# First head pair of a clustered attention and mixture kernel: centroid norms by Newton steps alone, identity matmuls in TensorE's pauses, seven exchange transfers, shared evictions, and GpSimd's split held back

## The chip, the cores and the metric

The kernel runs on one core of one Trainium2 chip. The metric is the device time of one execution in microseconds; where several runs are given, the median counts. The core's engines work from queues of their own: TensorE (PE; its weight loads are shown as PEld), VectorE (DVE), ScalarE (ACT), GpSimd (POOL) and SyncE (SP), which here only issues transfers. ScalarE and GpSimd can issue transfers too.

## What is computed

Inputs are q, k, v of shape (2, 8, 768, 64), 16 centroids per head, and the weights of two feed-forward stages. The attention lets a query see a key only if both fall into the same cluster:

```python
q_n = q / (norm(q) + 1e-06)
k_n = k / (norm(k) + 1e-06)
c_n = centroids / (norm(centroids) + 1e-06)
q_assign = argmax(einsum('bhsd,hcd->bhsc', q_n, c_n), -1)
k_assign = argmax(einsum('bhsd,hcd->bhsc', k_n, c_n), -1)
mask = q_assign[:, :, :, None] == k_assign[:, :, None, :]
scores = where(mask, scale * q @ k.T, -1e9)
attn = softmax(scores)
x = (attn @ v) reshaped to (1536, 512)
x = leaky_relu(x @ w_in) @ w_out
out = gated mixture of 8 experts on x, with a skip gate
```

An argmax over clusters does not depend on the length of q or k, so the kernel normalizes the centroids only.

## The kernel before

The attention works on eight pairs (a batch and two heads each), with 12 steps per pair in a software pipeline of 96 steps (the loop `for s in range(NSTEP + 12 + LAG)`). A step takes 128 queries of one head: `st_scores` makes the 128x768 scores on TensorE (tile `sps`), VectorE takes the row maximum (`st`), ScalarE the exponential (`pr`), TensorE transposes it (`tps`), ScalarE evicts that (`pt`), and a few steps later TensorE multiplies by v (`avps`). Scores have nearly f32 accuracy from operands split into a high and a low part. For the first head of a pair they lie in U = `UA` and V = `VA`, for the second in `UB` and `VB`; each tile has 128 partitions and a q and a k part. In U the high part stands in partitions 0 to 63 and the cluster mask, 16 rows of large numbers, from 64 on; V holds the parts for the two correction products. Since the two heads of a pair arrive in different partition halves, parts move between halves by transfers in SBUF: the exchange.

The preparation of a pair: transposes of the loaded q and k on TensorE (`raw_pe`, tile `rawps`), evictions (`raw_act`, tile `raw`), the cluster scores (`assign_pe`, tile `asps`), their eviction (`sc`), transposes (`argmax_pe`, tile `scps`), four VectorE passes for a one-hot of the argmax (`argmax_0` to `argmax_3`: `mx`, `eq`, `eq`, `mx`, `oh`), and the mask rows. For later pairs a table (`plan`, `PREPS`) spreads these over the steps of the pair before. For pair 0 there is nothing to hide behind: it is written out in line ahead of the step loop, and each engine's queue has the order in which these statements stand. That is where nearly all of the change lies.

Before, in this opening: SyncE issues the loads of q (tile `first`), the centroids (`cnat`), k (`first`), then q and k of pair 1. `first_copy` brings q and k into the layout for the transposes, one half on ScalarE, the other on VectorE (q) or GpSimd (k). `prep_centroids` takes the norms: square (`csq`), sum, a square root on ScalarE, two Newton steps on VectorE, reciprocal, and the scaled centroids (`cexp`); `prep_cblk` transposes these on TensorE (`cps`) and copies them to `cblk`, the weights of `asps`. `first_hi` makes the high parts (GpSimd for q, ScalarE for k), `first_lo` the low parts (VectorE). Then the exchange, nine transfers of 192 KB, eight on SyncE's queue and one on GpSimd's. `mask_first` makes the mask rows by 24 small transposes (`mps`), evicted by ScalarE (keys) and VectorE (queries). Pair 1 is transposed and evicted during the argmax; `split_first(1, i)` splits it on GpSimd and starts its exchange.

Of the kernel before, what the change touches and what calls it, by code (L numbers as in the profile page):

```python
# [25 lines left out]
def kernel(  # L26
# [14 lines left out]
    nc = tc.nc  # L41
# [51 lines left out]
    def load_qk(p):  # L93
        b, cc = divmod(p, NPAIR)
        for nm, src in (("q", q), ("k", k)):
            if p:
                t = att_a.tile([P, NT, 2, D], F32, tag="nat" + nm, name="nat" + nm)
                nat[nm, p] = t
                nc.sync.dma_start(t, src[b, 2 * cc:2 * cc + 2].rearrange("h (p t) d -> p t h d", t=NT))
            else:  # L100
                t = att.tile([P, 2, HS], F32R, tag="pr", name="first", bufs=4)
                t = _f(t.rearrange("p a b -> p (a b)")).rearrange("p (h t d) -> p h t d", h=2, d=D)
                nc.sync.dma_start(t, src[b, 0:2].rearrange("h (p t) d -> p h t d", t=NT))
                first[nm] = t
                nat[nm, 0] = nat0[:, "qk".index(nm)]
            if p == 0 and nm == "q":
                nc.sync.dma_start(cnat, centroids.rearrange("h c d -> (h c) d"))

# [27 lines left out]
    nc.vector.memset(warm, 1.0)  # L136
    nc.scalar.activation(out=warm, in_=warm, func=AF.Sqrt)
    nc.vector.tensor_single_scalar(pid, pid, NC_, op=ALU.bitwise_and)
# [4 lines left out]
    def prep_centroids():  # L143
# [3 lines left out]
        nc.vector.tensor_reduce(out=st[:, 0:1], in_=sq, axis=AX.X, op=ALU.add)  # L147
        first_copy(1)
        nc.scalar.activation(out=st[:, 1:2], in_=st[:, 0:1], func=AF.Sqrt)
        nc.vector.tensor_scalar(out=st[:, 1:2], in0=st[:, 1:2], scalar1=1e-30, scalar2=None, op0=ALU.max)  # L150
        for i in (1, 2):
            nc.vector.reciprocal(out=st[:, 3:4], in_=st[:, i:i + 1])
            nc.vector.scalar_tensor_tensor(out=st[:, 3:4], in0=st[:, 0:1], scalar=st[:, 3:4], in1=st[:, i:i + 1],
                                           op0=ALU.mult, op1=ALU.add)
            nc.vector.tensor_scalar(out=st[:, 2 * i:2 * i + 1], in0=st[:, 3:4], scalar1=0.5, scalar2=1e-6 * (i - 1),
                                    op0=ALU.mult, op1=ALU.add)
# [30 lines left out]
    def raw_act(p, i):  # L187
        qk, half = divmod(i, 2)
        ps = ps_prep.pop(("raw", i)).rearrange("p j c -> p (j c)")
        sc = SCALE if qk == 0 else 1.0  # L190
        nc.scalar.activation(out=raw_t[p][:, i, :], in_=ps, func=AF.Copy, scale=sc)

# [8 lines left out]
    def raw_split(p, i):  # L201
# [5 lines left out]
        lo = (VA if qk == 0 else VB)[:, qk, cs]  # L207
        nc.gpsimd.tensor_scalar(out=hi, in0=raw[:, i, :], scalar1=1.0, scalar2=1.0, op0=ALU.mult, op1=ALU.mult)
        nc.gpsimd.tensor_tensor(out=lo, in0=raw[:, i, :], in1=_f(hi), op=ALU.subtract)
# [57 lines left out]
    def argmax_3(p):  # L267
# [3 lines left out]
        oh_t[p] = oh  # L271

    def mask_first(h):
        U = uv_t[0][h]
        for qk in (1, 0):
# [8 lines left out]
            else:  # L284
                for cs in (slice(0, HS), slice(HS, S)) if h == 0 else (slice(0, S),):
                    nc.vector.tensor_scalar(out=U[64:64 + NC_, 0, cs], in0=ps[:, cs], scalar1=BIG, scalar2=-BIG,
                                            op0=ALU.mult, op1=ALU.add)

# [180 lines left out]
    def first_copy(i):  # L469
        nm = "qk"[i // 2]  # L470
        ts_ = slice(3 * (i % 2), 3 * (i % 2) + 3)
        for h in range(2):
            src, dst = first[nm][:, h, ts_, :], nat[nm, 0][:, ts_, h, :]
            if h:
                nc.scalar.activation(out=dst, in_=src, func=AF.Copy)
            elif nm == "q":
                nc.vector.tensor_copy(dst, src)
            else:
                nc.gpsimd.tensor_scalar(out=dst, in0=src, scalar1=1.0, scalar2=1.0, op0=ALU.mult, op1=ALU.mult)

    first_copy(0)
    prep_centroids()
    first_copy(2)
    first_copy(3)
    for i in range(4):
        raw_pe(0, i)
        raw_act(0, i)
    for i in range(4):
# [4 lines left out]

    def first_lo(qk, halves=(0, 1)):
        for half in halves:
            cs = slice(half * HS, (half + 1) * HS)
# [3 lines left out]
    Uq, Wq, Xq, Yq = (_f(t[:, 0, :]) for t in (UA, UB, VA, VB))  # L500
    Uk, Wk, Xk, Yk = (_f(t[:, 1, :]) for t in (UA, UB, VA, VB))
    nc.sync.dma_start(Wq[0:64], Uq[64:128])
    nc.sync.dma_start(Yq[64:128], Uq[64:128])
    nc.sync.dma_start(Wk[0:64], Uk[64:128])
    nc.sync.dma_start(Yk[0:64], Uk[64:128])
    first_lo(0, (0,))
    prep_cblk()
    first_lo(0, (1,))
    nc.sync.dma_start(Yq[0:64], Xq[64:128])
    nc.gpsimd.dma_start(Xk[0:64], Uk[0:64])  # L510
    assign_pe(0)
    first_lo(1)
    lo_kf = _f(lo_k.rearrange("p a b -> p (a b)"))
    nc.sync.dma_start(Xk[64:128], lo_kf[0:64])
    nc.sync.dma_start(Yk[64:128], lo_kf[64:128])
    nc.sync.dma_start(Xq[64:128], Uq[0:64])
    prep(0, 3, "a0")
    nc.scalar.activation(out=warm, in_=warm, func=AF.Exp)
    prep(0, 3, "pb")
    for r in range(4, 7):  # L520
        for slot in ("d", "pb"):
            prep(0, r, slot)
    load_v(0)
    for i in range(4):
        raw_pe(1, i)
        raw_act(1, i)
    load_qk(2)
    mask_first(0)
# [160 lines left out]
    for s in range(NSTEP + 12 + LAG):  # L689
        p, r = divmod(s, 12)  # L690
        if s < NSTEP:
            st_scores(s)
        conv_step(s, 0)
        preps(p, r, "a0")
# [929 lines left out]
```

## Time and profile before

| | us |
|---|---|
| median of 3 runs | 648.55 |
| lowest and highest | 646.94, 648.65 |
| the profiled execution's own time | 648.61 |
| its span, first to last instruction | 646.9 |
| TensorE busy in it | 626.0 |
| VectorE, ScalarE, GpSimd busy | 481.5, 415.5, 164.1 |

The profile is of one execution. Its times count from the start of the span. In a timeline a line is a group of like instructions that follow each other: start, time from the first start to the last end, engine, source line, operation, what it writes and reads, the number of instructions, and the idle time before it with what ended it. In the chain of waits a line is a piece of the path that ended last: start, length, engine or transfer, and the source line.

### The profile page before, as it was taken

The page shows a single profiled execution, that of the slowest core. Times are in us where ns is not written, and L with a number is a line of the kernel's source. Part 1 is how long each engine was busy: PE and PEld are TensorE (multiplying, and loading weights), DVE is VectorE, ACT ScalarE, POOL GpSimd, SP SyncE. Part 2 cuts the span into 40 slices and gives each one's busy share as a digit, 9 for nine tenths or more (in the row PEclk, how much of TensorE's full clock was granted, in tenths as well). Part 3 has the DMA queues.
Part 4 walks back from the last instruction along what each step waited for, and adds up shares of the span by engine and source line. Part 5 has one row for each costly group of instructions (what it writes and reads, how often), then busy time and mean ns, then how long its engine had stood idle before and what let it go on. Part 6 is the DMA issues. An engine that isn't in the chain of part 4 may idle for free.

```text
span 646.9 us, 10034 instructions
## 1 busy us (share of the span) xinstructions
PE 626.0 (97%) x3505; PEld 485.7 (75%) x3505; DVE 481.5 (74%) x893; ACT 415.5 (64%) x817; POOL 164.1 (25%) x215
## 2 busy tenths in 40 slices
PE   5999999999999999999999999999998999999994
PEld 3776777776776775888888888888886878688874
DVE  6757778787868653988766888767988548999961
ACT  5788898988888885655544444445453346688860
POOL 3333647463746333400000000000000125005111
PEclk9999999999999999999999999999998999999998
DMA  7766566578666518233014211017353438999940
GB/s 187 181 188 169 137 158 196 150 198 188 193 185 165 169 33 315 79 117 98 3 35 146 98 42 39 17 50 261 133 195 126 141 131 305 368 362 363 359 137 28
DMA packets 66246, 104.26 MB, mean 161 GB/s; under 512 B 27994, under 2 KB 32060, under 8 KB 65810
## 3 DMA queue, kind: packets, MB, share of 16 engines
q1 hardware_dynamic: 62914, 95.36, 47.5%
q0 software_dynamic: 3280, 8.24, 3.9%
q8 instruction: 28, 0.46, 0.3%
q14 instruction: 24, 0.20, 0.1%
HBM read 77.45 MB, written 12.72 MB: 139 GB/s over the span
## 4 chain that ended last, share of the span: by engine, by line
PE 83%; DVE 7%; ACT 3%; DMA 2%; POOL 2%; issue 2%; SPq 0%; POOLq 0%; DVEq 0%
PE ups L669 17%; PE acc L775 16%; PE sps L371 10%; PE avps L443 9%; PE tps L428 8%; PE hps L1315 7%; PE yps L1346 7%; DVE ohe L881 2%; PE rawps L179 1%; ACT pr L389 1%; PE hT L1327 1%; PE acc L1207 1%; PE asps L232 1%; DVE gl L762 1%; DMA stg<-in_moe_w_in_dram 1%
## 5 line engine op out<-in xcount | busy, mean ns | idle before, releaser
L374 DVE TENSOR_REDUCE st<-sps 128x1 f32<-128x768 f32 x96 | 91.6, 955 | 52.2 <-PE sps L371 51.2
L435 ACT ACTIVATE pt<-tps 128x384 f32<-128x384 f32 x192 | 85.4, 509 | 18.6 <-PE tps L428 17.4
L389 ACT ACTIVATE pr<-sps,st 128x768 f32<-128x768 f32 x96 | 87.9, 916 | 10.0 <-DVE st L374 9.8
L428 PE MATMUL tps<-ident,pr 128*128 128x128 f32 x576 | 79.1, 273 | 0.5 <-ACT pt L435 0.5
L669 PE MATMUL ups<-xh,whii 128*128 128x512 f32 x192 | 74.9, 390 | 0.0
L669 PE MATMUL ups<-xh,wloi 128*128 128x512 f32 x192 | 74.7, 389 | 0.0
L669 PE MATMUL ups<-xl,whii 128*128 128x512 f32 x192 | 74.7, 389 | 0.0
L775 PE MATMUL acc<-whio,gh 128*128 128x512 f32 x183 | 72.8, 398 | 0.0
L428 PEld LDWEIGHTS tps<-ident,pr 128*128 128x128 f32 x576 | 67.8, 140 | 5.9 <-ACT pt L435 1.8
L443 PE MATMUL avps<-pt,vnat 128*64 128x384 f32 x384 | 72.1, 498 | 0.0
L775 PE MATMUL acc<-whio,gl 128*128 128x512 f32 x183 | 71.7, 392 | 0.0
L775 PE MATMUL acc<-wloo,gh 128*128 128x512 f32 x183 | 71.7, 392 | 0.0
L760 ACT ACTIVATE gh<-g 128x512 fp32r<-128x512 f32 x48 | 30.4, 633 | 59.5 <-DVE g L759 59.5
L758 ACT ACTIVATE lk<-ups 128x512 f32<-128x512 f32 x48 | 28.4, 592 | 40.7 <-PE ups L669 35.7
L762 DVE TENSOR_TENSOR gl<-g,gh 128x512 fp32r<-128x512 f32 x48 | 33.2, 691 | 25.2 <-ACT gh L760 25.2
L1047 POOL DMA_INDIRECT xe<-x_scratch,eix x1 | 1.2, 1167 | 190.6 <-PE ups L669 190.6
L881 DVE SCALAR_TENSOR_TENSOR ohe<-x,x2Ts 128x512 f32<-128x512 f32 x63 | 43.5, 690 | 1.5
L759 DVE TENSOR_TENSOR g<-ups,lk 128x512 f32<-128x512 f32 x48 | 33.0, 688 | 15.3 <-ACT lk L758 14.8
L443 PEld LDWEIGHTS avps<-pt,vnat 128*64 128x64 f32 x384 | 23.5, 136 | 25.5 <-issue 25.1
L669 PEld LDWEIGHTS ups<-xh,whii 128*128 128x128 f32 x192 | 36.0, 188 | 8.0 <-issue 0.6
L669 PEld LDWEIGHTS ups<-xh,wloi 128*128 128x128 f32 x192 | 36.1, 188 | 7.6
L669 PEld LDWEIGHTS ups<-xl,whii 128*128 128x128 f32 x192 | 36.0, 188 | 7.4
(312 smaller groups left out, 1366.1 us busy)
## 6 DMA issues: line engine op xcount, KB each, us to landing
rawb<-in_moe_w_dram SPq DMA_DIRECT2D x25, 1024.0 KB
rawa<-in_moe_w_dram SPq DMA_DIRECT2D x10, 1024.0 KB
stg<-in_moe_w_in_dram SPq DMA_DIRECT2D x16, 512.0 KB
stg<-in_moe_w_out_dram SPq DMA_DIRECT2D x16, 512.0 KB
x2Ts<-gate_scratch SPq DMA_DIRECT2D x18, 256.0 KB
UB<-UA SPq DMA_DIRECT2D x16, 192.0 KB
vnat<-in_v_dram SPq DMA_DIRECT2D x8, 384.0 KB
rb<-recip_scratch POOLq DMA_DIRECT2D x32, 96.0 KB, 2.8
```

The costliest lines, as they stand in the source:

```text
L371: nc.tensor.matmul(ps[:, kh, 0:HS], lhsT=t[0:n, 0, qs], rhs=t[0:n, 1, kh * HS:(kh + 1) * HS], start=first, stop=not first)
L374: nc.vector.tensor_reduce(out=st[:, 0:1], in_=ps[:, :, 0:HS], axis=AX.XY, op=ALU.max, negate=True)
L389: nc.scalar.activation(out=pr, in_=ps[:, :, 0:HS], func=AF.Exp, bias=st[:, 0:1], accum_out=sm_t[g][:, 3 * h + j:3 * h + j + 1])
L428: nc.tensor.transpose(ps[:, t, :], pr[:, kh, t * P:(t + 1) * P], ident)
L435: nc.scalar.activation(out=pt[:, 3 * kh:3 * kh + 3, j, :], in_=t_t[s][kh], func=AF.Copy)
L443: nc.tensor.matmul(av_t[g][64 * h:64 * h + 64, :], lhsT=vnat[p][:, h, kt, :], rhs=pt_t[p, half, h][:, kt].rearrange("p j c -> p (j c)"), s ...
L669: nc.tensor.matmul(ps, lhsT=w[:, cc, :], rhs=x[:, blk, cc, :], start=(n == 0), stop=(n == 3 * KD - 1))
L762: nc.vector.tensor_tensor(out=gl, in0=g, in1=_f(gh), op=ALU.subtract)
L775: nc.tensor.matmul(ps, lhsT=a[:, ts_], rhs=w, start=(fc == 0 and n == 0), stop=(fc == NFC - 1 and n == 2))
L881: nc.vector.scalar_tensor_tensor(out=junk[0].rearrange("p t n -> p (t n)"), in0=x2_t[blk, t // 2][:, t % 2, :], scalar=1.0, in1=wgb_t[blk, ...
L1315: nc.tensor.matmul(ps, lhsT=x[:, c, :], rhs=w, start=(n == 0), stop=(n == len(mm) - 1))
L1346: nc.tensor.matmul(ps[:, cs], lhsT=x[:, f, :], rhs=w[:, cs], start=(h == 0 and f == 0 and n == 0), stop=(h == 1 and f == 3 and n == 2))
```

## The change

Five things change, all in the opening of pair 0 but for the second halves of the masks, which move into steps 1 and 2.

- The centroids' load goes to ScalarE's queue. The table that ScalarE loads at the start is now that of the exponential; the square root is replaced by a start value from integer operations on the number's bits and three Newton steps on VectorE.
- q's copies go from VectorE to GpSimd. The evictions of the second halves of q and k of pair 0 go from ScalarE to VectorE. `prep_cblk` stands ahead of the fourth set of transposes.
- `warm_pe(n)` issues n f32 matmuls of the identity with itself into a tile `wps` that nothing reads: 7 at the start, 3 ahead of `asps`, 2 ahead of `scps`, 5 ahead of and 5 after the last transposes of pair 1.
- Two of the nine transfers become ScalarE copies within the same partitions, one goes to ScalarE's queue. v's load stands behind pair 1's transposes.
- The first instruction of GpSimd's split of pair 1 reads its factor 1.0 from a tile `hold`, which VectorE fills after the argmax.

```diff
-                nc.sync.dma_start(cnat, centroids.rearrange("h c d -> (h c) d"))
+                nc.scalar.dma_start(cnat, centroids.rearrange("h c d -> (h c) d"))
...
-    nc.scalar.activation(out=warm, in_=warm, func=AF.Sqrt)
+    nc.scalar.activation(out=warm, in_=warm, func=AF.Exp)
+    hold = const.tile([P, 1], F32, name="hold")
...
-        first_copy(1)
-        nc.scalar.activation(out=st[:, 1:2], in_=st[:, 0:1], func=AF.Sqrt)
-        nc.vector.tensor_scalar(out=st[:, 1:2], in0=st[:, 1:2], scalar1=1e-30, scalar2=None, op0=ALU.max)
-        for i in (1, 2):
+        si = st.bitcast(I32)
+        nc.vector.tensor_single_scalar(si[:, 1:2], si[:, 0:1], 1, op=ALU.logical_shift_right)
+        nc.vector.tensor_scalar(out=si[:, 1:2], in0=si[:, 1:2], scalar1=float(0x1FBD1DF5), scalar2=None, op0=ALU.add)
+        for i, j in ((1, 2), (2, 5), (5, 4)):
...
+        if p == 0 and half:
+            nc.vector.tensor_scalar(out=raw_t[p][:, i, :], in0=ps, scalar1=sc, scalar2=None, op0=ALU.mult)
+            return
         nc.scalar.activation(out=raw_t[p][:, i, :], in_=ps, func=AF.Copy, scale=sc)
...
-        nc.gpsimd.tensor_scalar(out=hi, in0=raw[:, i, :], scalar1=1.0, scalar2=1.0, op0=ALU.mult, op1=ALU.mult)
+        nc.gpsimd.tensor_scalar(out=hi, in0=raw[:, i, :], scalar1=hold if p == 1 and i == 0 else 1.0, scalar2=1.0,
+                                op0=ALU.mult, op1=ALU.mult)
...
+    def mask_query(h, half):
+        cs = slice(half * HS, (half + 1) * HS)
+        nc.vector.tensor_scalar(out=uv_t[0][h][64:64 + NC_, 0, cs], in0=mq_t[h][:, cs], scalar1=BIG, scalar2=-BIG,
+                                op0=ALU.mult, op1=ALU.add)
...
-                for cs in (slice(0, HS), slice(HS, S)) if h == 0 else (slice(0, S),):
-                    nc.vector.tensor_scalar(out=U[64:64 + NC_, 0, cs], in0=ps[:, cs], scalar1=BIG, scalar2=-BIG,
-                                            op0=ALU.mult, op1=ALU.add)
+                mq_t[h] = ps
+                mask_query(h, 0)
...
-            elif nm == "q":
-                nc.vector.tensor_copy(dst, src)
...
-    first_copy(0)
+    wps = ps_s("wps")[:, 0, 0:P]
+
+    def warm_pe(n):
+        for _ in range(n):
+            nc.tensor.matmul(wps, lhsT=ident, rhs=ident, start=True, stop=True)
+
+    warm_pe(7)
     prep_centroids()
-    first_copy(2)
-    first_copy(3)
     for i in range(4):
+        first_copy(i)
+    for i in range(3):
         raw_pe(0, i)
-        raw_act(0, i)
+    raw_act(0, 0)
+    raw_act(0, 1)
+    prep_cblk()
+    raw_pe(0, 3)
+    raw_act(0, 2)
+    raw_act(0, 3)
+    warm_pe(3)
+    assign_pe(0)
+    warm_pe(2)
...
     nc.sync.dma_start(Wq[0:64], Uq[64:128])
-    nc.sync.dma_start(Yq[64:128], Uq[64:128])
+    first_lo(0)
+    nc.sync.dma_start(Yq[0:64], Xq[64:128])
     nc.sync.dma_start(Wk[0:64], Uk[64:128])
     nc.sync.dma_start(Yk[0:64], Uk[64:128])
-    first_lo(0, (0,))
-    prep_cblk()
-    first_lo(0, (1,))
-    nc.sync.dma_start(Yq[0:64], Xq[64:128])
-    nc.gpsimd.dma_start(Xk[0:64], Uk[0:64])
-    assign_pe(0)
     first_lo(1)
-    lo_kf = _f(lo_k.rearrange("p a b -> p (a b)"))
     nc.sync.dma_start(Xk[64:128], lo_kf[0:64])
     nc.sync.dma_start(Yk[64:128], lo_kf[64:128])
-    nc.sync.dma_start(Xq[64:128], Uq[0:64])
     prep(0, 3, "a0")
-    nc.scalar.activation(out=warm, in_=warm, func=AF.Exp)
     prep(0, 3, "pb")
+    nc.scalar.activation(out=VA[0:64, 1, :], in_=Uk[0:64], func=AF.Copy)
+    nc.scalar.activation(out=VB[64:128, 0, :], in_=Uq[64:128], func=AF.Copy)
+    nc.scalar.dma_start(Xq[64:128], Uq[0:64])
     for r in range(4, 7):
         for slot in ("d", "pb"):
             prep(0, r, slot)
-    load_v(0)
+    nc.vector.memset(hold, 1.0)
     for i in range(4):
         raw_pe(1, i)
         raw_act(1, i)
+        if i > 1:
+            warm_pe(5)
+    load_v(0)
...
+        if 1 <= s < 3:
+            mask_query(s - 1, 1)
```

How the instructions stand in the queues is shown at three places. The first is TensorE from the start to the one-hot transposes of `mps`; before:

```order
L179 MATMUL rawps<-ident,nat_87 128x128 x12
L164 MATMUL cps<-ident,cexp 128x128
L232 MATMUL asps<-raw,cblk 32x384 x4
L244 MATMUL scps<-ident,sc 128x128 x3
L179 MATMUL rawps<-ident,natq 128x128 x6
L179 MATMUL rawps<-ident,natk 128x128 x6
```

and with the change:

```order
L494 MATMUL wps<-ident 128x128 x7
L180 MATMUL rawps<-ident,nat_87 128x128 x9
L165 MATMUL cps<-ident,cexp 128x128
L180 MATMUL rawps<-ident,nat_87 128x128 x3
L494 MATMUL wps<-ident 128x128 x3
L237 MATMUL asps<-raw,cblk 32x384 x4
L494 MATMUL wps<-ident 128x128 x2
L249 MATMUL scps<-ident,sc 128x128 x3
L180 MATMUL rawps<-ident,natq 128x128 x6
L180 MATMUL rawps<-ident,natk 128x128 x3
L494 MATMUL wps<-ident 128x128 x5
L180 MATMUL rawps<-ident,natk 128x128 x3
```

The centroids' transpose moves ahead of the last three transposes of pair 0, and 22 matmuls on `wps` stand in between (a further five follow the last row, ahead of `mps`).

The second is SyncE's queue from its first transfer in SBUF to v's load (a tile name with B on the left and A on the right is a move from one head's tile to the other's); before:

```order
L502 DMA UB<-UA 64x768
L503 DMA VB<-UA 64x768
L504 DMA UB<-UA 64x768
L505 DMA VB<-UA 64x768
L509 DMA VB<-VA 64x768
L514 DMA VA<-lo_k 64x768
L515 DMA VB<-lo_k 64x768
L516 DMA VA<-UA 64x768
L112 DMA vnat<-in_v_dram 128x2x384
```

and with the change:

```order
L526 DMA UB<-UA 64x768
L528 DMA VB<-VA 64x768
L529 DMA UB<-UA 64x768
L530 DMA VB<-UA 64x768
L532 DMA VA<-lo_k 64x768
L533 DMA VB<-lo_k 64x768
L112 DMA vnat<-in_v_dram 128x2x384
```

Six transfers of the exchange are left here; the low part of q moves from fifth to second place.

The third is ScalarE after the start; before:

```order
L191 ACTIVATE raw<-rawps 128x384 x4
L197 ACTIVATE UA<-raw 128x384 x2
L238 ACTIVATE sc<-asps 128x384
L518 ACT_TABLE_LOAD
L518 ACTIVATE warm<-warm 128x1
L191 ACTIVATE raw<-rawps 128x384 x4
L283 ACTIVATE UA<-mps 16x768
```

and with the change:

```order
L195 ACTIVATE raw<-rawps 128x384 x2
L201 ACTIVATE UA<-raw 128x384 x2
L243 ACTIVATE sc<-asps 128x384
L536 ACTIVATE VA<-UA 64x768
L537 ACTIVATE VB<-UA 64x768
L538 DMA VA<-UA 64x768
L195 ACTIVATE raw<-rawps 128x384 x4
L295 ACTIVATE UA<-mps 16x768
```

Two evictions of pair 0 and the table load are gone from here; two copies and the seventh transfer stand between the eviction of `asps` and pair 1's evictions.

## Rows read from the trace of the kernel before

**Rows 1.** The page: busy time of each engine, and the chain by engine.

```profile
PE 626.0 (97%) x3505; PEld 485.7 (75%) x3505; DVE 481.5 (74%) x893; ACT 415.5 (64%) x817; POOL 164.1 (25%) x215
...
PE 83%; DVE 7%; ACT 3%; DMA 2%; POOL 2%; issue 2%; SPq 0%; POOLq 0%; DVEq 0%
```

**Rows 2.** Stretch: length, busy of PE, PEld, DVE, ACT, POOL, clock, DMA share, GB/s.

```profile
60.00:100.00 40.00, 40.00 (x273) 28.46 (x272) 29.98 (x45) 35.80 (x85) 20.19 (x28) 1.00 0.61 162
```

**Rows 3.** Chain of waits, 0 to 40 us: start, length, what.

```profile
1.81 4.74 DMA first<-in_k_dram
...
9.38 1.57 PE asps L232 x8
...
11.52 0.91 PE scps L244 x3
...
16.11 2.73 PE mps L280 x24
18.84 1.59 PE sps L371 x4
...
20.45 0.97 DVE st L374
...
27.18 0.97 PE sps L371 x4
```

**Rows 4.** Timeline of TensorE: the same forms early and late, and a plain f32 matmul.

```profile
4.33 1.52 PE L179 MATMUL rawps<-ident,nat 128*128 128x128 f32 x6 [4.33 <-DVE csq L146]
...
9.38 1.51 PE L232 MATMUL asps<-raw,cblk 128*32 128x384 f32 x8 [0.54 <-DVE cblk L165]
...
21.18 0.85 PE L232 MATMUL asps<-raw,cblk 128*32 128x384 f32 x8
...
23.75 0.55 PE L244 MATMUL scps<-ident,sc 128*128 128x128 f32 x3 [0.29 <-ACT sc L238]
...
24.84 0.82 PE L428 MATMUL tps<-ident,pr 128*128 128x128 f32 x6
...
528.67 1.58 PE L1068 MATMUL xT<-ohe,x 128*128 128x128 f32 x12
```

**Rows 5.** Stretches before and after the clock changes, columns as in rows 2.

```profile
17.20:20.50 3.30, 3.30 (x21) 3.09 (x19) 2.03 (x4) 1.36 (x2) 3.13 (x5) 1.00 0.91 235
...
491.60:495.00 3.40, 1.38 (x7) 0.88 (x7) 2.64 (x9) 2.11 (x4) 0.00 (x0) 1.00 0.03 10
495.00:498.40 3.40, 3.11 (x11) 2.52 (x11) 2.67 (x7) 0.79 (x3) 0.00 (x0) 0.51 0.00 0
```

**Rows 6.** Timeline of VectorE in the opening, and the second pair's oh.

```profile
1.41 0.30 DVE L85 CAST identb<-ident 128x128 bf16<-128x128 f32 x1 [1.41 <-POOL ident masks.py:199]
...
4.10 0.21 DVE L146 TENSOR_TENSOR csq<-cnat 128x64 f32<-128x64 f32 x1
...
6.51 0.58 DVE L159 TENSOR_SCALAR cexp<-cnat,cst,par 128x64 f32<-128x64 f32 x2
...
14.82 1.24 DVE L269 TENSOR_TENSOR oh<-eq,mx 128x384 bf16<-128x384 f32 x1
17.59 1.03 DVE L286 TENSOR_SCALAR UA<-mps 16x384 fp32r<-16x384 bf16 x2 [1.54 <-PE mps L280]
...
30.84 0.55 DVE L269 TENSOR_TENSOR oh<-eq,mx 128x384 bf16<-128x384 f32 x1
```

**Rows 7.** Timeline of GpSimd: the split of pair 1 during oh.

```profile
15.62 0.81 POOL L208 TENSOR_SCALAR UA<-raw 128x384 fp32r<-128x384 f32 x1
```

**Rows 8.** Stretches of the loads and of the exchange, columns as in rows 2.

```profile
9.70:18.70 9.00, 7.24 (x47) 5.50 (x39) 5.43 (x10) 5.48 (x10) 5.48 (x7) 1.00 0.93 204
2.50:3.50 1.00, 0.00 (x0) 0.00 (x0) 0.20 (x2) 0.00 (x0) 0.00 (x0) 1.00 1.04 325
3.50:4.50 1.00, 0.17 (x1) 0.20 (x2) 0.64 (x4) 0.62 (x2) 0.00 (x0) 1.00 0.75 174
```

**Rows 9.** Timeline of ScalarE: a mask eviction.

```profile
16.95 0.80 ACT L283 ACTIVATE UA<-mps 16x768 fp32r<-16x768 bf16 x1 [1.45 <-PE mps L280]
```

More of the change, by code (lines that the diff above doesn't have):

```diff
@@ L154, in prep_centroids @@
                                            op0=ALU.mult, op1=ALU.add)
-            nc.vector.tensor_scalar(out=st[:, 2 * i:2 * i + 1], in0=st[:, 3:4], scalar1=0.5, scalar2=1e-6 * (i - 1),
+            nc.vector.tensor_scalar(out=st[:, j:j + 1], in0=st[:, 3:4], scalar1=0.5, scalar2=1e-6 if j == 4 else 0.0,
                                     op0=ALU.mult, op1=ALU.add)
@@ L271, in argmax_3 @@
         oh_t[p] = oh
+    mq_t = {}
+    def mask_query(h, half):
+        cs = slice(half * HS, (half + 1) * HS)
+        nc.vector.tensor_scalar(out=uv_t[0][h][64:64 + NC_, 0, cs], in0=mq_t[h][:, cs], scalar1=BIG, scalar2=-BIG,
+                                op0=ALU.mult, op1=ALU.add)
     def mask_first(h):
@@ L492, with first_lo @@
     lo_k = att.tile([P, 2, HS], F32R, tag="pr", name="lo_k", bufs=4)
-    def first_lo(qk, halves=(0, 1)):
-        for half in halves:
+    def first_lo(qk):
+        for half in range(2):
             cs = slice(half * HS, (half + 1) * HS)
@@ L501 @@
     Uk, Wk, Xk, Yk = (_f(t[:, 1, :]) for t in (UA, UB, VA, VB))
+    lo_kf = _f(lo_k.rearrange("p a b -> p (a b)"))
     nc.sync.dma_start(Wq[0:64], Uq[64:128])
-    nc.sync.dma_start(Yq[64:128], Uq[64:128])
+    first_lo(0)
+    nc.sync.dma_start(Yq[0:64], Xq[64:128])
     nc.sync.dma_start(Wk[0:64], Uk[64:128])
     nc.sync.dma_start(Yk[0:64], Uk[64:128])
-    first_lo(0, (0,))
-    prep_cblk()
-    first_lo(0, (1,))
-    nc.sync.dma_start(Yq[0:64], Xq[64:128])
-    nc.gpsimd.dma_start(Xk[0:64], Uk[0:64])
-    assign_pe(0)
     first_lo(1)
-    lo_kf = _f(lo_k.rearrange("p a b -> p (a b)"))
     nc.sync.dma_start(Xk[64:128], lo_kf[0:64])
     nc.sync.dma_start(Yk[64:128], lo_kf[64:128])
-    nc.sync.dma_start(Xq[64:128], Uq[0:64])
     prep(0, 3, "a0")
-    nc.scalar.activation(out=warm, in_=warm, func=AF.Exp)
     prep(0, 3, "pb")
+    nc.scalar.activation(out=VA[0:64, 1, :], in_=Uk[0:64], func=AF.Copy)
+    nc.scalar.activation(out=VB[64:128, 0, :], in_=Uq[64:128], func=AF.Copy)
+    nc.scalar.dma_start(Xq[64:128], Uq[0:64])
     for r in range(4, 7):
```

## The prediction

> **What bounds the kernel now.** I read the page first: TensorE is busy for 97% of the span, and the chain that ended last is 83% TensorE [rows 1]. Then the busy time by stretches: between 60 and 100 us TensorE is busy all 40.00 us [rows 2]. So from the step loop on TensorE is the limit, and whatever delays the loop's first steps delays the end by as much. The change works almost wholly ahead of that, so I read the chain of waits of the opening [rows 3]. It runs: k's first load lands at 6.55 us (issued at 1.81, 4.74 later); copies, transposes, evictions; cluster scores (asps) 9.38 to 10.95; transposed scores (scps) 11.52; the argmax on VectorE until 16.06 [rows 6]; the one-hot transposes (mps) 16.11 to 18.84; the first step's scores (sps) until 20.43; the first row maximum (st) at 20.45. That 20.45 is the mark I count with: what it loses, the end loses.
>
> Two things in this chain are slower than they are later. TensorE: six f32 transposes take 1.52 us at 4.33 but 0.82 at 24.84; asps takes 1.51 us at 9.38 (1.57 in the chain) but 0.85 at 21.18, scps 0.91 but 0.55 at 23.75 [rows 3, 4], and the four sps matmuls 1.59 but 0.97 at 27.18. The granted clock in the opening's rows reads 1.00, yet these durations are those of the lower level, 1.2 GHz: at 495.00 to 498.40 the clock is 0.51, after a stretch in which TensorE was busy for 1.38 of 3.40 us [rows 5]. By the durations it rises in the opening at the end of a stretch in which TensorE was busy throughout, 17.20 to 20.50 [rows 5]; from there on the forms have their later durations. VectorE: the last argmax step (oh) takes 1.24 us at 14.82 and 0.55 at 30.84 [rows 6]; a GpSimd split of the second pair, itself slow at 0.81 us, runs across its end [rows 7].
>
> The third resource is the exchange: nine transfers of 192 KB between partition halves, 1.77 MB. In 9.70 to 18.70 the DMA engines have a share of 0.93 at 204 GB/s, 1.84 MB with the start of v's load [rows 8]. So a transfer costs 1.0 us of all engines, and the exchange ends together with mps: the two paths are nearly tied.
>
> **The change, part by part.**
>
> *Centroids' load on ScalarE's queue, k's load one issue earlier.* k is issued at 1.31 instead of 1.81. Between 2.5 and 3.5 us the engines move 325 GB/s, between 3.5 and 4.5 only 174 at a share of 0.75 [rows 8]: k's bytes came late and were then shared with the loads behind them. Bounds for k's landing: 0.5 earlier (the issue alone) to 1.3 earlier (the hole closed as well); I take 0.9, so 5.65, since the hole lies just where k's bytes were due. The Trainium skill, "Trainium Kernel Development and Optimization", section Key Constraints, says that issuing from several engines saves only issue time, as all queues run on the same 16 DMA engines; by that k would land only 0.5 earlier and the sum would be up to 0.4 us higher.
>
> *Norms by Newton steps.* ScalarE's square root and the floor go, two integer operations and a third Newton step come. Before, csq to the end of the scaled centroids ran from 4.10 to 7.09 with a copy in between [rows 6]; now I count sixteen small operations (four more, some 0.2 us each; the copy is gone), 3.6 us at most, from the centroids' landing. With them landing at 3.3 (bounds 2.9 and 4.1) cexp is ready at 6.9. It sits beside k's landing, copies and transposes (5.65 to 6.9); at 4.1 it would be late by 0.8 and asps with it.
>
> *q copies on GpSimd, half the evictions on VectorE, cps ahead of the last transposes.* GpSimd has no other work there. cps at 6.95, the last three transposes until 7.9, VectorE evicts them by 8.6. The three fillers behind them: a plain f32 128x128 matmul is two records; twelve records take 1.58 us at the higher level, some 1.44 without the last one's tail [rows 4], 0.24 a matmul; at the lower level I take 0.45. Three are 1.35, so asps starts at 9.2 instead of 9.38: **-0.2**. Without the fillers it would start at 8.7; this is their price if the clock is still low. asps itself keeps its length in my likeliest case.
>
> *The clock.* Seven fillers, from the identity at 1.41 [rows 6] until 4.5, hide behind q's load. From 7 us on TensorE now hardly pauses: transposes, three fillers, asps, two fillers, scps. A stretch as full as 17.20 to 20.50 [rows 5] thus comes some 7 us earlier, and I take the clock to rise around 11 us, at scps. Then scps costs 0.55 instead of 0.91: **-0.36**. The two fillers in front of it lie beside ScalarE's copy of asps.
>
> *GpSimd's split held until oh is done.* oh at 0.55 instead of 1.24: **-0.69**. The first four argmax steps keep their length. The split then runs some 1 us later in absolute time; what waits for it is the second pair's exchange, needed in step 12, some 20 us after the mark, and it costs nothing there.
>
> *Fillers beside the argmax.* In front of mps stand nine transposes, five fillers, three transposes that wait for ScalarE's eviction, five fillers. ScalarE has two new copies before that eviction, nearest row 0.80 us for a 16x768 eviction [rows 9], and an issue. At the higher level that queue ends about 0.6 us after oh: **+0.6**.
>
> *mps and sps.* At half the time mps is 2.73/2, **-1.35**, and sps 0.97 instead of 1.59, **-0.62** [rows 3].
>
> *Masks in halves.* The second query halves move behind the row maxima of steps 1 and 2. VectorE waits there for TensorE; half a mask is 0.52 us (two in 1.03 at 17.59 [rows 6]) and the cover is the pause between the second and third maximum. Zero, or up to 0.5 in one step if that cover goes.
>
> *Seven transfers.* Two become ScalarE copies within a partition. 7.0 us of engine time, first bytes about 9.5, so the last lands at about 16.6, before mps ends (about 16.7). Zero, now that TensorE is earlier too; but it caps larger gains. The removed table load had only evictions of the second pair behind it: zero.
>
> Sum: -0.2 - 0.36 - 0.69 + 0.6 - 1.35 - 0.62 = -2.6 us. The profiled execution took 648.61 us (span 646.9), the median of the runs is 648.55; against either the forecast is **646.0 us**.
>
> **Rivals.**
>
> *A, the clock rises already before asps (0.25).* For it: the seven fillers alone are 3 us of plain matmuls. Against it: TensorE then pauses for k. If so, asps costs 0.85 and the fillers half; mps could end at 15.4 and the transfers become the limit: the second step's scores cannot be done much before 17.5, the second maximum moves from 21.42 to 17.6. Gain 3.8: 644.8 us.
>
> *B, transposes do not raise it (0.2).* Between 7.09 and 15 us TensorE worked mostly on transposes at the lower level and the clock stayed there; in 17.20 to 20.50 it had sps matmuls too. If only plain matmuls count, the rise comes between 13.8 and 16.4, among the ten fillers, which then cost 0.45 each until it. mps starts 1.2 to 2.5 us later than in the forecast: gain 0.2 to 1.6, 647.0 to 648.4. The Trainium skill, "TensorE: Matmul & The Clock Gate", Part 4, says this of transposes: they do not count as busy in the same way. By that rule the time would be in this rival's band; the rows before 15 us agree with it, but mps, also transposes, fills half of the stretch after which it rose.
>
> *C, the exchange does not start earlier (0.08).* Its first transfer waits for both q halves. If these come as late as before (9.70 first bytes) and the last one, behind ScalarE's copies, collides with v's load, the last landing is 17.0 rather than 18.7: gain 1.6, 647.0.
>
> *D, slower: the clock stays low through all fillers (0.05).* Then the queue ahead of mps at 12.3 is 2.7 us of transposes, two times five fillers at 0.45 and the wait: mps starts at about 19.2, is 2.73 long, and the maximum comes at 23.5, 3 us late: 651.6. It decides at a rise near 16.5; earlier it is B. Against it: by then TensorE would have worked without a pause for longer than it had before the rise in the run above [rows 5].
>
> That the change does nothing is the edge of B and C.
>
> **How the numbers follow.** The forecast has 0.42. Its own spread is k's landing (0.8), the centroids' (0.8) and the filler wait: 645.0 to 646.9. Low end: A less half a microsecond, and the runs themselves: they go from 646.94 to 648.65, and a run without the half-clock stretch at 495.00 would, as an estimate from its 3.40 us at 0.51, be 1.7 us shorter. If two of three such runs fall together the median is lower by as much. High end: most of B. **643.8 to 648.0** leaves out D, the edge of B and a lucky A. About 0.3% (1.95 us) is what can be told from no change: faster means below 646.6. Faster 0.62 (four fifths of the forecast's cases, A, and a little of B and C), within 0.3% 0.33, slower 0.05.
>
> **What would show it.** In the changed profile: k copied by ScalarE near 5.7 us; asps at 9.2 or before; scps in 0.55 and mps in about 1.4; oh in 0.55; first row maximum near 17.8, and from there the old spacing of the maxima. Wrong if mps still takes 2.7 us (B, D), if mps starts over 1 us after oh, if sps waits for a landing (C, A's limit), or if the maxima of steps 2 and 3 fall behind the old spacing because of the mask halves, or if the gain at the first maximum is not found at step 12.

## The result, and the profile after

The change made the kernel slower: 654.60 us (median of four runs, 653.61 to 657.19) against 648.41 for the kernel before beside it, a ratio of 1.0107 (95% interval 1.0081 to 1.0133). 646.0 was predicted, with a range to 648.0. The profiled execution took 653.61 us, span 651.9.

The opening reached its mark as forecast. TensorE's timeline after, columns as in [rows 4]; `x14` are the seven fillers, two records each:

```profile
1.43 3.35 PE L494 MATMUL wps<-ident 128*128 128x128 f32 x14 [1.43 <-POOL ident masks.py:199]
...
8.74 0.88 PE L237 MATMUL asps<-raw,cblk 128*32 128x384 f32 x8
...
10.23 0.55 PE L249 MATMUL scps<-ident,sc 128*128 128x128 f32 x3
...
13.49 0.55 PE L180 MATMUL rawps<-ident,natk 128*128 128x128 f32 x3 [0.61 <-ACT raw L195]
13.87 1.28 PE L494 MATMUL wps<-ident 128*128 128x128 f32 x10
15.08 1.51 PE L292 MATMUL mps<-identb,oh 128*16 128x128 bf16 x24
16.72 0.59 PE L382 MATMUL sps<-UA 80*128 80x384 f32 x2
```

VectorE's timeline after:

```profile
13.18 0.56 DVE L274 TENSOR_TENSOR oh<-eq,mx 128x384 bf16<-128x384 f32 x1
...
17.85 1.82 DVE L385 TENSOR_REDUCE st<-sps 128x1 f32<-128x768 f32 x2 [0.67 <-PE sps L382]
...
255.02 0.68 DVE L783 TENSOR_TENSOR g<-ups,lk 128x512 f32<-128x512 f32 x1
...
260.11 0.68 DVE L783 TENSOR_TENSOR g<-ups,lk 128x512 f32<-128x512 f32 x1
```

asps takes 0.88 us and scps 0.55 (1.57 and 0.91 in [rows 3]), oh 0.56 (1.24 in [rows 6]), and the first row maximum starts at 17.85, not 20.45: 2.60 earlier. The lead holds through the whole step loop (2.55 at its end). Then the feed-forward stage begins. It takes 512 tokens of the attention's output (`xh`, `xl`) through blocks of the first weights (`whii`, `wloi`) into PSUM tiles `ups`, 12 matmuls of 128x512 a block; VectorE takes a leaky maximum (`g`), ScalarE and VectorE split it (`gh`, `gl`), and 12 matmuls with the second weights (`whio`, `wloo`) add to four tiles `acc`. TensorE makes three blocks of `ups` ahead of the first `acc`. Before:

```profile
253.52 0.50 PE L669 MATMUL ups<-xh,whii 128*128 128x512 f32 x1
...
261.83 0.39 PE L775 MATMUL acc<-whio,gh 128*128 128x512 f32 x1
```

and after:

```profile
250.97 0.50 PE L691 MATMUL ups<-xh,whii 128*128 128x512 f32 x1
...
260.84 0.50 PE L691 MATMUL ups<-xh,whii 128*128 128x512 f32 x1 [4.01 <-DVE g L783]
...
261.83 0.63 PE L691 MATMUL ups<-xh,whii 128*128 128x512 f32 x1
...
265.29 0.40 PE L799 MATMUL acc<-whio,gh 128*128 128x512 f32 x1
```

TensorE stands 4.01 us ahead of the third block, until VectorE's second `g` at 260.11; behind that the matmuls last 0.63 us each instead of 0.40, and `acc` starts 3.46 later than before. A lead of 2.55 has become a lag of 3.46. The stretch behind the pause, columns as in [rows 2], shows the clock at half:

```profile
261.40:264.80 3.40, 3.40 (x9) 2.67 (x8) 1.99 (x3) 1.66 (x4) 2.15 (x12) 0.50 0.00 0
```

A second loss has no pause. Between 300 and 400 us TensorE is busy for all 100 us at full clock in both kernels, but gets through 438 matmuls where it did 445. Before, then after:

```profile
300.00:400.00 100.00, 100.00 (x445) 82.75 (x444) 76.71 (x151) 46.51 (x81) 0.53 (x1) 1.00 0.21 67
```

```profile
300.00:400.00 100.00, 100.00 (x438) 81.51 (x438) 76.37 (x149) 46.51 (x81) 0.53 (x1) 1.00 0.21 66
```

It is the `ups` matmuls: twelve take 2.79 us instead of 2.72, while twelve `acc` take 2.73 and 2.72. Over the 46 blocks behind the pause that is some 3.3 us. The two losses are 6.8 us, the profiled span grew by 5.0: the half-clock stretch of before at 495 us [rows 5], which the prediction put at 1.7 us, is not in the changed profile. The page's groups say the same, mean ns of one before and after:

```profile
L669 PE MATMUL ups<-xh,whii 128*128 128x512 f32 x192 | 74.9, 390 | 0.0
```

```profile
L691 PE MATMUL ups<-xh,whii 128*128 128x512 f32 x192 | 76.8, 400 | 4.0 <-DVE g L783 4.0
```

### The profile page after: what moved, and what is told of

The parts are those of the page before. It is cut to its first block, busy times and chain, and to the rows that moved or that the text cites. A ratio compares the mean times of both kernels' runs of the same rounds, so it can differ in the third digit from the quotient of the medians.

```text
span 651.9 us, 10123 instructions
## 1 busy us (share of the span) xinstructions
PE 632.3 (97%) x3549; PEld 488.7 (75%) x3549; DVE 484.9 (74%) x899; ACT 415.6 (64%) x814; POOL 163.7 (25%) x216
## 4 chain that ended last, share of the span: by engine, by line
PE 80%; DVE 9%; DMA 3%; ACT 3%; issue 2%; POOL 1%; SPq 0%; POOLq 0%; ACTq 0%; DVEq 0%
PE ups L691 17%; PE acc L799 16%; PE sps L382 9%; PE avps L454 8%; PE tps L439 7%; PE hps L1339 7%; PE yps L1370 7%; DVE ohe L905 2%; PE rawps L180 1%; DMA rb<-recip_scratch 1%; ACT pr L400 1%; PE hT L1351 1%; PE acc L1231 1%; DVE g L783 1%; DVE wloo L678 1%
## 5 line engine op out<-in xcount | busy, mean ns | idle before, releaser
L691 PE MATMUL ups<-xh,whii 128*128 128x512 f32 x192 | 76.8, 400 | 4.0 <-DVE g L783 4.0
L691 PE MATMUL ups<-xh,wloi 128*128 128x512 f32 x192 | 76.7, 400 | 0.0
L691 PE MATMUL ups<-xl,whii 128*128 128x512 f32 x192 | 76.4, 398 | 0.0
```

The source lines that it names most:

```text
L691: nc.tensor.matmul(ps, lhsT=w[:, cc, :], rhs=x[:, blk, cc, :], start=(n == 0), stop=(n == 3 * KD - 1))
```

## The experiments

Ratios are to the kernel before, run beside each, with 95% intervals.

### The pause: where the PSUM tiles lie

Each kind of PSUM tile gets its banks when its first tile is allocated. Before, the order was transposes (T, banks 0 and 1), M, A and then the scores' kind S (4 to 7). `wps` is of kind S and the first of all, so after the change S has banks 0 to 3 and T 4 and 5. The first two `ups` are made in two S tiles of two banks each, the third in bank 0 of a new pool. Before, bank 0 was a free bank of T. After the change it is half of the S tile whose other half, bank 1, holds the second `ups`; the new pool waits for the tile as a whole, until `g` has been read from it. That gives theory 1; `e1_layout` puts the kinds back, `e2_before_sfirst` moves them in the kernel before, `e3_bank_order` hands out the new pool's banks in another order.

```diff
+    for _ in range(2):
+        ps_t([P, 3, P], "place")
+    ps_m([P, 3, P], "place")
+    ps_a([P, 3, P], "place")
     ident = const.tile([P, P], F32, name="ident")
```

> The change, with four PSUM tiles that nothing writes allocated at its top, so that the kinds of PSUM tile lie in the banks they have in the kernel before; no instruction is added. Theory 1 (the filler's tile is the first tile of PSUM, it moves the step loop's banks, and the third group of up matmuls then waits for VectorE's second max): TensorE does not stand at the start of the feed-forward stage, 36 up matmuls run there without a pause, later groups of 12 take 2.72 us and not 2.79, and the time is the one before less the 2.55 us that the loop starts earlier, 645.8 us (644.5 to 646.5). Theory 2 (an earlier loop meets the same late transfers and operations, so that TensorE stands there whatever the banks are): the pause of about 4.0 us stays and the time stays at 653.5 to 655.5. Theory 3 (the pause goes but the slower spacing of the up matmuls has a cause of its own): 648 to 650.

Measured: 650.05 us, 1.0040 (1.0022 to 1.0058). TensorE's timeline: the third block of `ups` follows at once, and a smaller wait is left ahead of the second `acc` tile, which gets bank 5, where the second `ups` lies in this order.

```profile
259.52 0.39 PE L804 MATMUL acc<-whio,gh 128*128 128x512 f32 x1
...
261.10 0.50 PE L804 MATMUL acc<-whio,gh 128*128 128x512 f32 x1 [0.73 <-DVE g L788]
...
263.28 0.39 PE L696 MATMUL ups<-xh,whii 128*128 128x512 f32 x1
```

```diff
# e2_before_sfirst, on the kernel before
+    ps_s("place")
     ident = const.tile([P, P], F32, name="ident")
```

> The kernel before, with one PSUM tile of the loop's kind that nothing writes allocated first, so that the banks lie as in the change; no instruction is added, and the opening is that of before. Theory 1: TensorE stands some 2.9 us before the third group of up matmuls (VectorE's second max is 261.6 to 262.3 us there, and the first two groups end at about 259.3), the clock falls as in the change (+1.9), and the later spacing adds about 3.4: 655 to 657 us, less up to 1.7 if the dip of before at 495 us goes. Theory 2: 648.4 us, no pause. Theory 3: a pause, but 2.72 us for 12 up matmuls: 651.5 to 653.5.

Measured: 651.75 us, 1.0054 (1.0027 to 1.0081). With before's opening and one unused tile the pause is there, and the slow matmuls after it; but 445 matmuls run between 300 and 400 us, as theory 3 has it.

```profile
261.97 0.50 PE L671 MATMUL ups<-xh,whii 128*128 128x512 f32 x1 [2.75 <-DVE g L761]
...
266.39 0.42 PE L777 MATMUL acc<-whio,gh 128*128 128x512 f32 x1
```

```diff
# e3_bank_order, on the change, ahead of the stage's first tiles
+    bank("misc", 1, "place")
+    bank("lg", 1, "place")
```

> The change with its own banks in the step loop, and in the feed-forward stage the banks handed out in another order (two others first), so that the third group of up matmuls lands on the banks of the first group's tile, which VectorE's first max has left by then. Theory 1: no pause of 4 us (at most 0.5), 645.5 to 647 us, as with the banks moved at the top. Theory 2: the pause stays, 653.5 to 655.5. Theory 3: no pause but 2.79 us for 12 up matmuls: 648 to 650.

Measured: 649.80 us, 1.0030 (1.0012 to 1.0048); no pause. And `e4_no_fillers`, the change without `wps` and every `warm_pe`:

> The change without its 22 identity matmuls and without their tile, so the banks lie nearly as before and the third group of up matmuls takes a free bank. Theory 1: no pause in the feed-forward stage; the opening loses what the fillers bought: the clock rises late, the assignment and the first scores run at 1.2 GHz as before, but nothing stands before the masks' matmuls (-1.3): 646.3 to 647.8 us, 0.5 to 2 more than with fillers and the banks put right. If the fillers buy nothing: 645.5 to 646. Theory 2: the loop starts earlier than before by 1 to 2 us all the same and the pause comes, over 651.

Measured: 649.94 us, 1.0030 (1.0014 to 1.0045); no pause, 438 matmuls in the stretch. So the banks made the pause (shown from both sides); it is worth some 4.5 of the 6.2 us (650.05 and 649.80 against 654.60). The spacing is something else: theory 3, and it came with neither banks nor fillers.

### The spacing: where the weights lie in SBUF

`hold` takes 32 bytes of SBUF, and the tiles placed behind it move on by as much, the weights' halves among them. `xh` and `xl`, placed from the other end of SBUF, stay.

```diff
# e5_layout_pad64, on e1_layout
-    hold = const.tile([P, 1], F32, name="hold")
+    hold = const.tile([P, 16], F32, name="hold")[:, 0:1]
```

> The change with the banks put right as in e1_layout, and the new small tile that holds GpSimd's split back made 64 bytes wide, where it took 32: all tiles behind it, the feed-forward weights' halves among them, move on by 32 bytes and stand modulo 64 as in the kernel before. Theory 4 (the slower spacing of the up matmuls comes from that shift by 32 bytes): 12 up matmuls take 2.72 us, and the time falls by some 3.3 us against e1_layout (46 groups by 0.07 us), to 645.3 to 647.0 us. Theory 5 (it comes from what runs beside TensorE, ScalarE and VectorE being ahead of it): 2.79 us as in e1_layout, 649.5 to 650.5.

Measured: 650.46 us, 1.0044 (1.0031 to 1.0057); 2.80 us for 12. That is a miss: a shift of 64 bytes is no better than one of 32.

```diff
# e6_before_pad32, on the kernel before
+    const.tile([P, 1], F32, name="pad")
```

> The kernel before with one unused tile of 32 bytes where the change has the tile that holds the split back; no instruction is added or moved. Theory 4: 12 up matmuls take 2.79 us from the first group on and the time is the one before plus 3.3 us, 650.5 to 652. Theory 5: 2.72 us and the time of before, 648.

Measured: 651.32 us, 1.0058 (1.0039 to 1.0076); 2.79 us from the first block on, and 438 in the stretch:

```profile
300.00:400.00 100.00, 100.00 (x438) 81.51 (x437) 75.62 (x148) 46.57 (x80) 0.53 (x1) 1.00 0.20 67
```

An unused tile of 32 bytes costs 3.9 us (647.41 beside it), all of the second loss. The next put 32 bytes ahead of `whii` and `wloi` alone (so these moved by 64, the rest by 32):

> The change with the banks put right, the small tile left at 32 bytes, and 32 unused bytes ahead of the halves of the up weights alone: of what the small tile had moved only these stand modulo 64 as in the kernel before. If the place of the stationary operand is what counts: 12 up matmuls in 2.72 us, 645.3 to 647.0. If another of the moved tiles (the transfers' buffers, the raw weights, what ScalarE and VectorE read) makes the difference: 2.79 us, 649.5 to 650.5.

Measured: 650.23 us, 1.0047 (1.0031 to 1.0062); 2.80 us. `e9_same_layout` brings every tile back:

```diff
# e9_same_layout, on e1_layout
-    warm = const.tile([P, 1], F32, name="warm")
+    warm2 = const.tile([P, 2], F32, name="warm")
+    warm, hold = warm2[:, 0:1], warm2[:, 1:2]
...
-    hold = const.tile([P, 1], F32, name="hold")
```

> The change with the banks put right as in e1_layout, and the value that holds GpSimd's split back kept in the second column of a small tile that is there anyway, so that every tile lies at the address it has in the kernel before. Theory 4a (the slower spacing comes with any move of the tiles, by 32 or by 64 bytes): 12 up matmuls take 2.72 us, and the time is the one before less what is left of the 2.55 us, 645.3 to 647.0 us. Theory 5 (what runs beside TensorE): 2.79 us and 649.5 to 650.5.

Measured: 648.13 us, 1.0009 (0.9990 to 1.0028); 2.72 us for 12. The spacing is as theory 4a has it, the time is not.

```profile
300.00:400.00 100.00, 100.00 (x445) 82.73 (x444) 76.96 (x152) 46.48 (x81) 0.53 (x1) 1.00 0.20 64
```

Which tile, and how far? The kernel before with unused bytes ahead of `whii` and `wloi` alone, one run each:

```diff
# e10_before_wpad32 (32 bytes); e11_before_wpad256 has [P, 64] (256 bytes)
             wip[0] = pool("wi", "left")
+            wip[0].tile([P, 8], F32, tag="pad", name="pad", bufs=1)
```

> The kernel before with 32 unused bytes ahead of the halves of the up weights alone, all else in its place; one look. If TensorE's reads of the stationary operand make the spacing: 2.79 us for 12 up matmuls, about 650.7 us. If another tile that moved in e6_before_pad32 does: 2.72 us, 645.5 to 650.

Measured: 651.50 us, 2.79 us for 12.

> The same with 256 unused bytes; one look. If what counts is the place within 256 bytes (in the kernel before the up weights and the activations stand alike modulo 256, after the change they do not): 2.72 us for 12. If any move of these tiles does it: 2.79 us.

Measured: 647.93 us, 2.72 us for 12, 445 in the stretch. So, by one profile each, the address of the weights' halves sets the spacing: moved by 32 or 64 bytes they are slow, by 256 or not at all fast. Before, they and `xh` start alike modulo 256 (224 both), and so do the two operands of `acc`, which no edit moved and whose twelve kept 2.72 to 2.75 us throughout. Whether that agreement is what counts was not tried (it would need `xh` moved alone).

### The lead that does not reach the end

With banks and addresses put right the change is no faster than before, though its first maximum comes at 17.78, 2.67 us earlier than in [rows 3]. Where does that go? `e8_nofill_pad64` is, despite its name, `e4_no_fillers` once more, without padding:

> A second look at the change without fillers, to see whether ScalarE's wait for GpSimd's split at 172 to 175 us (2.65 us with the banks in another order, 0.30 in the change, though their loops are alike) comes and goes by itself. If it belongs to the kernel: again over 2 us. If by chance: anything between 0.3 and 2.7. The time stays at 649 to 651 either way.

Measured: 650.01 us, and ScalarE's wait is there again, 2.95 us in both: in this kernel it seems to be the rule. `e12_same_act`, ScalarE's two copies and its transfer moved behind the third eviction of pair 1:

> e9_same_layout with ScalarE's two copies and the transfer it issues moved behind the third eviction of the second head pair's rotated tiles. If the late start of the masks' matmuls (1.3 us after the one-hots) comes from ScalarE's order (the fourth rotation waits 0.6 us for the first eviction, and ten identity matmuls stand behind it): they start 0.5 to 0.8 us earlier, and the time is that of e9_same_layout less 0.5 or, if the transfer is then late for the second step's scores, as much more.

Measured: 650.41 us, 1.0034 (1.0012 to 1.0057). mps starts at 14.23, 0.84 earlier, but the second scores then wait for the transfer:

```profile
17.90 0.59 PE L387 MATMUL sps<-VA 128*128 128x384 f32 x2 [1.10 <-DMA VA<-UA]
```

The first maximum comes at 18.53 (17.78 without the move). Behind these pauses the granted clock is 0.66 between 20.40 and 23.80, where `e9_same_layout` has 1.00, and the third maximum is 1.42 late (22.25 against 20.83). The order of the change was the better one.

From the first maximum to the first `ups` the loop takes 233.07 to 233.58 us in some profiles (before 233.07, after 233.12, `e9_same_layout` 233.58) and 234.02 to 234.95 in others (`e2_before_sfirst` 234.38, `e3_bank_order` 234.84, `e10_before_wpad32` 234.95), of either kernel. ScalarE's timeline of `e3_bank_order`, whose loop is the change's own:

```profile
175.48 0.49 ACT L195 ACTIVATE raw<-rawps 128x384 f32<-128x384 f32 x1 [2.65 <-POOL VB L214]
```

The same wait was 0.30 in the change. In seven of the ten long loops it is over 2.4 us, in the short ones at most 1.57; why `e2_before_sfirst` (1.31), `e5_layout_pad64` (0.30) and `e7_layout_wpad` (1.62) are long as well was not sought. GpSimd comes late because it waits for the store of the softmax's reciprocals (2.85 us here, 1.35 in the change), which on SP's queue stands behind the load of v:

```profile
155.70 2.80 SPq L112 DMA_DIRECT2D vnat<-in_v_dram  x1
...
159.89 0.32 SPq L728 DMA_DIRECT2D recip_scratch<-rrow  x1
```

And at the end of the loop `e9_same_layout` still waits:

```profile
261.63 0.50 PE L804 MATMUL acc<-whio,gh 128*128 128x512 f32 x1 [1.11 <-DVE g L788]
```

The reciprocals of the first half of the last pair (the next expectation says "the last pair but one") land 8 to 9 us after the issue of their load, behind three loads of 1 MB; GpSimd, ScalarE and VectorE are late by it. In the change:

```profile
240.06 1.10 POOL L425 DMA_DIRECT2D rb<-recip_scratch  x2 [1.91 <-DMA recip_scratch<-rrow]
249.30 0.99 POOL L468 TENSOR_TENSOR xr<-xr,rb 128x384 f32<-128x384 f32 x1 [8.14 <-DMA rb<-recip_scratch]
```

Two shifts of transfers take these waits away:

```diff
-            for c in range(NDIR // 4, NPC // 4):
-                load_f32(c)
             load_next(2)
...
+        if s == NSTEP + 5:
+            for c in range(NDIR // 4, NPC // 4):
+                load_f32(c)
# e14, e15, e17, e18 also
-        if r == 10 and p + 1 < NP:
+        if r == 11 and p + 1 < NP:
             load_v(p + 1)
```

> e9_same_layout with the three 1 MB loads of converted weights issued by SP five steps later, behind the last store of reciprocals. If the start of the feed-forward stage is set by the landing of the reciprocals of the last pair but one (8.5 us behind these loads, then GpSimd's split, ScalarE's eviction and split, VectorE's first and second max): GpSimd's split starts 1.5 to 2 us earlier there, TensorE does not stand on VectorE's second max (1.1 us before), and the time is 1.0 to 1.6 us under e9_same_layout, about 646.8. If not, e.g. since the loads are then late for the fifth group's weights: no gain, 648 to 651.

Measured: 646.57 us, 0.9986 (0.9971 to 1.0002); its interval overlaps that of `e9_same_layout`. In its profile GpSimd starts at 247.42 and no longer waits for the landing but for ScalarE, and TensorE doesn't stand:

```profile
247.42 1.00 POOL L473 TENSOR_TENSOR xr<-xr,rb 128x384 f32<-128x384 f32 x1 [6.31 <-ACT xr L467]
```

> The same, with the load of the next head pair's v behind the store of the reciprocals on SP's queue instead of ahead of it (its issue took 2.8 to 4.8 us there, and the store waited). If the lead of the loop is lost there (GpSimd late with the third pair's splits at 172 to 175 us): ScalarE's wait for the split at 172 us is under 0.5 us, the first up matmul is at 251.0 to 251.5 in every profile, and the median is another 1 us lower, about 645.8. If the lead is lost by chance elsewhere: as e13_same_late.

Measured: 645.75 us, 0.9971 (0.9957 to 0.9984), and in its repeat (`e18_same_late_v_again`) 645.74, 0.9974 (0.9959 to 0.9990). ScalarE's wait at 172 us is gone (0.24 and 0.38 in `e18` and `e17`); the loops of the four profiles with this shift take 232.74 to 233.31. The first `ups` is not always at 251 (251.58 and 252.29), since the openings differ. In `e18` the centroids come late, near the prediction's bound (`csq` at 4.06, in the change at 3.41); TensorE stands 1.58 us for `cexp`, the granted clock is 0.67 between 6.80 and 10.20, and asps takes 1.36 us.

```profile
172.86 0.50 ACT L200 ACTIVATE raw<-rawps 128x384 f32<-128x384 f32 x1
```

> The kernel before with the same two shifts of transfers. If the change's gain in the opening reaches the end once these transfers are out of the way: 2 to 2.5 us above e14_same_late_v, 647.5 to 648.2. If the transfers bound both alike: the two within 0.7 us.

Measured: 646.40 us, 0.9981 (0.9971 to 0.9990). The kernel before gains nearly as much: 0.65 us lie between the two, less than their intervals. So the opening is not worth 2.5 us. How much it is worth is blurred by half-clock stretches like that of [rows 5], which come in some executions only: one of these eleven runs has a mean granted clock under 0.996, but six of the twelve of `e14_same_late_v`. Without these the medians are 646.26 and 645.02, 1.2 us apart; the first maxima of the two profiles are 0.99 apart. The profile says why it is not more; TensorE's and VectorE's timelines:

```profile
13.06 1.49 PE L179 MATMUL rawps<-ident,natk 128*128 128x128 f32 x6
15.68 1.51 PE L280 MATMUL mps<-identb,oh 128*16 128x128 bf16 x24 [1.14 <-DVE oh L269]
...
19.42 1.82 DVE L374 TENSOR_REDUCE st<-sps 128x1 f32<-128x768 f32 x2 [0.96 <-PE sps L371]
```

With the opening of before mps takes 1.51 us here, not the 2.73 of [rows 3], and so it does in the four other profiles of that opening (`e2`, `e6`, `e10`, `e11`). In these five the first maximum lies at 19.10 to 19.63, not at 20.45.

### What the fillers buy

There are 22 fillers in all, the last five ahead of `mps` included. `e16_nofill_late_v` has, against its name, the transfers of `e9_same_layout`; `e17_nofill_best` has both shifts and ran beside `e18_same_late_v_again`.

> The change without its 22 identity matmuls and their tile, every SBUF tile at the address of before, transfers as in e9_same_layout. 12 up matmuls take 2.72 us. If the fillers buy what the prediction said they do (clock up before the masks' matmuls and the first scores): 0.5 to 1.5 above e9_same_layout. If ten fillers between the one-hots and the masks' matmuls cost as much as the clock gives: the same within 0.5.

Measured: 646.88 us, 0.9980 (0.9963 to 0.9996): lower than `e9_same_layout` (648.13, not run beside it), which neither case had.

> e14_same_late_v without the 22 identity matmuls and their tile (tiles of PSUM nearly as before, SBUF as before, both shifts of transfers). If the clock that the fillers raise before the masks' matmuls and the first scores reaches the end: 0.5 to 1.5 us above e18. If what they give at the clock they take by standing ahead of the masks' matmuls, or if it is lost in the loop: within 0.5 us of it.

Measured: 645.66 us, 0.9967 (0.9954 to 0.9980), against 645.74. The fillers buy nothing that can be measured. Without them asps is slow, but the clock is up by scps (in `e8_nofill_pad64` only behind it), and mps starts as early as with them (15.08 in the change, 16.35 in `e18_same_late_v_again`):

```profile
8.66 2.20 PE L237 MATMUL asps<-raw,cblk 128*32 128x384 f32 x8
11.45 0.55 PE L249 MATMUL scps<-ident,sc 128*128 128x128 f32 x3 [0.58 <-ACT sc L243]
...
15.01 1.51 PE L292 MATMUL mps<-identb,oh 128*16 128x128 bf16 x24 [0.36 <-DVE warm L533]
```

`e17_nofill_best` and `e14_same_late_v` are faster than both kernels, by about 0.3% than the one before; the first is the simpler. The shifted transfers alone (`e15_before_late_v`) bring 0.2%.

## Why the prediction was wrong, point by point

- **"What it loses, the end loses"** is the step that failed, and with it a term that was put at nothing without a reason: the place of the two new tiles. The mark came out, -2.60 against -2.6 at the first maximum, and still -2.55 at the first `ups`. But the sum priced instructions only. `wps`, which nothing reads, and the 32 bytes of `hold` moved other tiles: about 4.5 us by the banks, 2 to 4 by the addresses (`e1` against `e9`, `e6` against before). Neither was among the rivals; the slower one, D, stood at 0.05 and for another mechanism.
- **That the mark came out so closely is luck.** Terms were off both ways: scps starts 1.29 earlier (0.2 taken), the wait between oh and mps is 1.29 longer (0.6 taken), and from the end of mps to the maximum it is 0.35 less (0.62 taken). Two sums of the rivals are also a little off: D's parts give 19.5 and not 19.2 for the start of mps, B's leave a gain of 0.1 to 1.4.
- **The clock.** Rival A came in this profile (asps 0.88, clock up ahead of it; in `e5`, `e14` and `e18` asps took 1.31 to 1.44). ScalarE's late eviction (TensorE waits 0.61 for it) and the five fillers behind the last transposes (1.28) ate its gain: mps starts 1.34 us after oh ends, where 0.6 was taken. ScalarE's other order in `e12_same_act` gave 0.84 of that back. Rival B does not fit `e15_before_late_v`: asps ended at 10.46, only transposes ran from 11.08, at the lower level until 14.55, and by 15.68 the clock had risen. The Trainium skill, "TensorE: Matmul & The Clock Gate", Part 4, would not count them in the same way; as far as they go, these rows don't agree.
- **mps -1.35, sps -0.62** were mis-sized at the base: [rows 3] are of one execution whose clock rose later than in the five others. Against those the change's 17.85 is 1.3 to 1.8 earlier, not 2.6, and other profiles of the changed opening have 17.70 to 18.98.
- **oh -0.69, scps -0.36**: right (0.56 and 0.55). oh takes 1.24 us in all six profiles with the opening of before and 0.56 in all fourteen with the changed one, which fits the split held back as its cause; no run moved that alone.
- **Loads.** k is copied at 5.58 (5.7 forecast), 1.0 earlier than in the profile before by an issue 0.5 earlier. Over all profiles the gain is smaller: 5.86 to 6.57 with the opening of before, 5.40 to 6.17 with the changed one, 0.76 between the medians. Whether more than the issue time was saved (the Trainium skill, "Trainium Kernel Development and Optimization", Key Constraints, allows no more) these runs do not settle.
- **"From the step loop on TensorE is the limit"** holds in shares, not for a shift of 2 us: GpSimd's splits at 172 us and the landing of the reciprocals at 249 are within that of being the limit, and took part of the lead until the two transfers were moved (1.0009 in `e9`, 0.9971 in `e14`).

## What to carry to other kernels

A new scratch tile is a change to every tile that is placed behind it: compare bank and address of all tiles and the waits that stand on reuse, in the last stage too, before pricing any instruction. Put a new tile into one that is there, as `e9_same_layout` does, or last (not tried here). And price clock terms from several executions: what one profile shows of when the clock rose may be its own.

## What the runs showed of the hardware

- The spacing of 128x512 matmuls at full clock depends on where the stationary operand lies in SBUF: 227 ns (2.72/12) at one address and 256 bytes on, 233 ns 32 or 64 bytes on (`e6`, `e10`, `e5` and `e7` against `e9` and `e11`). The Trainium skill, "SBUF — State Buffer", section on the two separate sides, lets TensorE wait for no other engine there; these runs do not test that, they show that the spacing went with the address under either opening.
- The clock fell to half behind a pause of 4.01 us in the change and one of 2.75 in `e2_before_sfirst`, at the start of the feed-forward stage (0.50 in 261.40 to 264.80 of the change); the twelve matmuls behind it took 4.45 and 4.42 us instead of 2.72.
- The run-to-run spread goes with the clock. The kernel before ran beside the experiments 134 times: the median is 646.8 us in the 56 runs with a mean granted clock of 0.996 or 0.997, and 648.4 in the 78 below. With both transfers moved (`e15`) ten of eleven runs have 0.996 or 0.997, and the eleven lie within 645.75 to 647.34, where those beside them go from 645.78 to 650.08. What the store behind v's load does to the spread is not shown apart from that: its issue waited for the load's, which took 1.37 to 4.82 us, and 0.39 with the order turned.
